# Batch 1's local attention by key sets of one alignment, with exponentials as the stationary operand

## The chip, the cores and the metric

The kernel runs on one core of a Trainium2 chip. The metric is the device time of one execution in microseconds (us), lower is better. The engines of a core are TensorE (PE, matrix products, with its weight loads counted apart as PEld), VectorE (DVE), ScalarE (ACT), GpSimd (POOL) and SyncE (SP). Each works through a queue of its own; POOL, SP and ACT also issue transfers (DMAs).

## What is computed

Eight batches of eight heads, 512 local and 32 global tokens a head, head size 64. Global queries attend to all 544 keys; a local query attends to the 32 global keys and to the local keys at most 32 positions away. The result, laid out as 4352 rows of 512, goes through a two-layer network with a quick GELU.

```python
k_all = concat([k_g, k_l]); v_all = concat([v_g, v_l])
out_g = softmax(q_g @ k_all.T / 8) @ v_all
s_ll = where(|i - j| <= 32, q_l @ k_l.T / 8, -1e9)
out_l = softmax(concat([q_l @ k_g.T / 8, s_ll])) @ v_all
x = concat([out_g, out_l]).transpose(0, 2, 1, 3).reshape(4352, 512)
h = x @ w_in                      # 512 -> 2048
out = (h * sigmoid(1.702 * h)) @ w_out
```

## The kernel before

**Units.** A "quad" is four heads of one batch (u = 0 or 1), one in each 32-partition row group of PE; a batch has two, `a` and `c`. The code runs in `tc.manual_schedule()` (line 54): every engine issues its instructions in the order in which the program text writes them. PSUM is two pools: `psS`, two tiles of two banks each (`spair`, line 288, always the same two), and `psP`, four single banks under one tag (line 61, `pbank`), which hold "hp" (first layer), "op" (second layer), "ov" (values) and others in turn; a bank is handed on when the last reader of its tile is done.

**Two ways of attention.** Batches 0 and 1 use `Quad` (line 294). Keys are in four windows of 128 (`WIN`, line 192), and the queries' columns are interleaved. `Tk` and `Tq` turn keys and queries on DVE, `ext` copies the global queries in, `S` forms scores (two rounds, 16 products each), `gg` and `K` the products with global keys, `X` and `XK` take exponentials on ACT, `M` multiplies by a mask on DVE, `ekUs` and `U` form three units of 512 columns (the row sums and two halves of the values) with values or ones as stationary operand, `Gm` the global queries' output, `R` and `XL` turn the sums and divide. Batches 2 to 7 use `Wide` (line 537). Here the values are the moving operand and the exponentials the stationary one. Keys are in sets that start at any multiple of 32, so `spread` (ACT, line 547) puts the turned keys into groups of 96 with 32 columns left free for the global keys, which `ext` (DVE, line 561) fills by transposes together with the global queries. `turn_v` (line 99) makes two shifted copies of the values by DMAs on SP, one for each other alignment. `S` takes 56 products a round, `UG` (line 597) 22 products a head into three "ov" banks, `RXG` (line 616) divides on DVE and turns the result into `xL` and `xG`.

**Order of the work.** Batch 0's attention and first layer come first (to 32.5 us). Then batch 0's second layer, 16 steps of four products (`osteps`, line 800; (t, f) is token tile t, quarter f of the 2048), is written out by hand with batch 1's attention between the steps (lines 804 to 851). Then batch 1's first layer (lines 856 to 878): 16 chunks of four 512-column products, each followed by a tanh on ACT (line 652) and a multiply on DVE (line 653); into it go the turning of batch 2's `a` quad, `turn_v(2)` and `a.S(0)`, `a.X(0)`. From then on `phase_o(i)` (line 880, the second layer of batch i with the next batch's attention) and `phase_h(i)` (line 940, a first layer) alternate. In `phase_o(1)` the `c` quad of batch 2 is turned too.

**Loads.** POOL issues them, mostly at the start in `load_rest` (line 258): batch 0's values, `w_in`, `w_out` in groups of four chunks, batch 1's queries and keys, part of batch 2's. After batch 0 come `load_v(2)`, the wide masks (`mask_rest`, `mask_blocks`, POOL) and `load(3)`. Batch 1's mask, `near_mask`, is made by four ACT copies in batch 0's first layer (`make_near`, line 209).

Of the kernel before, what the change touches and what calls it, by code (L numbers as in the profile page):

```python
# [20 lines left out]
def kernel(  # L21
# [67 lines left out]
    def load_v(b):  # L89
        vt = v_rows(b)  # L90
        if b < 4:
            nc.gpsimd.memset(vt[:, :, :, D:], 1.0)
# [4 lines left out]
        nc.gpsimd.dma_start(out=vt[0:32, 5, :, :D], in_=vs[480:512])  # L97

# [11 lines left out]
    rvg = consts.tile([128, 4, D + 2], BF16)  # L110


    rvt = consts.tile([128, 4, D + 2], BF16)
# [5 lines left out]
    def load_g(lo, hi, names="kqv"):  # L119
        for name, dst, src in (("k", rkg, kgf), ("q", rqg, qgf)):  # L120
            if name in names:
                nc.gpsimd.dma_start(out=dst[:, lo:hi, :], in_=src[:, lo:hi, :])
        if "v" in names:
            load_turned(nc.gpsimd, rvg[:, lo:hi, :D], vgf[:, lo:hi, :])
# [36 lines left out]
    for i in range(2):  # L161
        vtiles.append(consts.tile([128, 8 * 6 * (D + 2)], BF16, name="v%d" % i))
        nc.gpsimd.memset(v_view(i, 4)[:, :, :, :, D:], 1.0)
# [22 lines left out]
    for i in range(4):  # L186
        qt = consts.tile([128, 24, 32], F32, name="q%d" % i)
        nc.vector.memset(qt[:, 0:4, :], 0.0)
        nc.vector.memset(qt[:, 20:24, :], 0.0)
# [3 lines left out]
    near_mask = consts.tile([128, 2, LW], BF16)  # L193
# [15 lines left out]
    def make_near(c):  # L209
        nr = WIN[c][1]  # L210
        at = (0, 160, 0, 192)[c]
        nc.scalar.activation(near_mask[:, c // 2, at : at + 16 * nr].rearrange("p (t r) -> p t r", t=16),
                             near(bandt, c), AF.Copy)

# [5 lines left out]
    def mask_put(g, first, last, by, late):  # L220
# [22 lines left out]
    qgT = consts.tile([128, 4, 40], F32)  # L243
    nc.vector.memset(qgT[:, :, 32:], 0.0)
    kgT = consts.tile([128, 4, 32], F32)
# [12 lines left out]
    def load_rest():  # L258
# [13 lines left out]
        load(1, (1,))  # L272
        load(2, kq=False)
        nc.gpsimd.dma_start(out=loaded[2][1][:, 0], in_=qf[2][:, 0])
        load_g(4, 8, "k")
        load_v2(1)
        load_g(4, 8, "q")
        nc.gpsimd.dma_start(out=loaded[2][0], in_=kf[2])
        nc.gpsimd.dma_start(out=loaded[2][1][:, 1], in_=qf[2][:, 1])
# [14 lines left out]
    class Quad:  # L294
        def __init__(self, Q):
# [5 lines left out]
            self.v = v_view(self.b, 4 if self.b < 2 else 5)[:, self.u]  # L301
            if self.b < 2:
# [43 lines left out]
        def S(self, rnd, split=False, added=False, part=None):  # L346
# [19 lines left out]
            if not part:  # L366
                self.E[rnd] = att.tile([128, 4, RW + 32], BF16, name="e%d" % rnd)
# [29 lines left out]
        def M(self, rnd):  # L397
            at = 36 if rnd else 40
            e = self.E[rnd][:, :, at : at + LW]
            nc.vector.tensor_mul(e, e, near_mask[:, rnd : rnd + 1, :].to_broadcast([128, 4, LW]))  # L400

# [25 lines left out]
        def XK(self, two=True):  # L427
            self.ek = att.tile([128, Sl], BF16, name="ek")
            nc.scalar.activation(self.ek, self.kb, AF.Exp, scale=scale)
            self.ek2 = None  # L430
            if two:
                self.ek2 = att.tile([128, Sl], BF16, name="ek2")
                load_turned(nc.sync, self.ek2, self.ek)

        def ekU(self, unit, warm=0, ov=None):
# [4 lines left out]
            for j in range(4):  # L440
                two = unit == 1 and self.ek2 is not None
                r = 32 * ((j + 1 + two) % 4)
                p = slice(r, r + 32)
                lv = (ones32[p] if unit == 0 else
                      (rvt if two else rvg)[p, self.Q, :D].rearrange("p (w h) -> p w h", h=2)[:, :, unit - 1])
                nc.tensor.matmul(ov[32 * j : 32 * j + 32, :], lhsT=lv, rhs=(self.ek2 if two else self.ek)[p],
                                 start=True, stop=False, skip_group_check=True)

        def ekUs(self, nxt=None, rnd=0, banks=(None, None, None)):
# [5 lines left out]
            if self.ek2 is not None:  # L455
                self.ekU(1, ov=banks[1])
            if nxt:
                nxt.K(1)
            if self.ek2 is None:
                self.ekU(1, ov=banks[1])  # L460
# [76 lines left out]
    class Wide(Quad):  # L537
# [30 lines left out]
        def S(self, rnd):  # L568
# [14 lines left out]
            self.E[rnd] = att.tile([128, 4, LW], BF16, name="e%d" % rnd)  # L583
# [13 lines left out]
        def UG(self):  # L597
            self.ov = []
            for lo, hi in self.BANKS:
                ov = pbank("ov")  # L600
                self.ov.append(ov)
                work = []
# [208 lines left out]
    a.S(0)  # L811
    a.gg()
    a.K()
    a.X(0)
    a.XK()
    a.M(0)
    a.eg()
# [177 lines left out]
```

## Time and profile before

| | us |
|---|---|
| three runs | 297.93, 302.67, 298.87 |
| their median | 298.87 |
| the profiled execution | 297.81 |
| its span, first to last instruction | 295.9 |
| batch 0's second layer with batch 1's attention | 32.45 to 53.64 |
| batch 1's first layer | 53.64 to 69.00 |
| phase_o(1) | 69.00 to 89.89 |
| phase_o(2), for comparison | 103.71 to 122.17 |

The profiled execution is 1.9 us longer than its span, and 1.06 us below the median of the runs. In the lines of a profile, L670 is line 670 of the kernel; "op<-w_out_sb,gT" is output from inputs by the program's names. "x12" counts instructions. In the page's groups the first time is the sum, the second the mean of one in ns, and behind the second bar stands the idle time ahead of them and what ended it. The chain of work that ended last has start, length and what ran, in order of time. The timeline has start, length, engine, line, operation, and in brackets idle time with its releaser.

### The profile page before, as it was taken

How to read it: one execution, taken by the hardware profiler on the slowest of the kernel's cores; microseconds unless marked ns; L12 is line 12 of the kernel's file. 1: busy time of each engine (PE TensorE's matmuls, PEld its weight loads, DVE VectorE, ACT ScalarE, POOL GpSimd, SP SyncE). 2: the span in 40 equal slices, each digit the busy share in tenths (PEclk: the TensorE clock that was granted, in tenths of full speed). 3: DMA queues.
4: the chain of work that ended last, by engine and by line, in shares of the span. 5: the costliest groups of instructions: out<-in, count | busy, mean ns of one | idle time of the engine just before them, and what ended most of it. 6: DMA issues, size and time to landing. Idle time of an engine off the chain costs nothing.

```text
span 295.9 us, 9633 instructions
## 1 busy us (share of the span) xinstructions
PE 286.8 (97%) x4129; PEld 145.2 (49%) x4129; DVE 200.6 (68%) x409; ACT 161.5 (55%) x282; POOL 81.9 (28%) x143
## 2 busy tenths in 40 slices
PE   7899999999899999999999999999999999999995
PEld 6454445444444455444554445445544454455553
DVE  6578957987867776787768768777678644773220
ACT  4838475485536746575546734765556551663421
POOL 8742754781933500910063003600000000000000
PEclk9999999999999999999999999999999999999999
DMA  6999999979999992996289213950226012101123
GB/s 191 177 207 210 204 181 231 132 155 206 132 194 218 224 155 65 124 208 144 50 100 208 51 40 55 172 143 12 64 58 182 2 42 70 38 0 35 40 56 86
DMA packets 62874, 35.94 MB, mean 121 GB/s; under 512 B 49776, under 2 KB 51184, under 8 KB 62832
## 3 DMA queue, kind: packets, MB, share of 16 engines
q0 software_dynamic: 52752, 17.77, 53.9%
q1 hardware_dynamic: 9600, 16.91, 20.9%
q8 instruction: 32, 0.52, 0.7%
q10 hardware_dynamic: 480, 0.66, 0.7%
q14 instruction: 10, 0.08, 0.1%
HBM read 36.70 MB, written 8.91 MB: 154 GB/s over the span
## 4 chain that ended last, share of the span: by engine, by line
PE 89%; DVE 4%; DMA 2%; ACT 2%; issue 1%; SPq 0%; ACTq 0%; DVEq 0%
PE hp L645 38%; PE op L670 38%; PE s L578 4%; PE ov L611 3%; DMA g32k<-in_k_g_dram 2%; PE s L645 1%; PE s L360 1%; DVE xL L505 1%; PE ov L472 1%; PE op L682 1%; ACT e L393 1%; DVE rs L500 0%; DVE gT L653 0%; DVE e L593 0%; DVE sT L496 0%
## 5 line engine op out<-in xcount | busy, mean ns | idle before, releaser
L670 PE MATMUL op<-w_out_sb,gT 128*128 128x512 bf16 x528 | 123.7, 380 | 0.0
L653 DVE SCALAR_TENSOR_TENSOR gT<-th,hp 128x512 bf16<-128x512 f32 (+1 forms) x140 | 90.5, 655 | 35.1 <-ACT th L652 34.0
L645 PE MATMUL hp<-xL,w_in_sb 128*128 128x512 bf16 x496 | 109.0, 379 | 0.3 <-DVE xL L505 0.2
L652 ACT ACTIVATE th<-hp 128x512 f32<-128x512 f32 (+1 forms) x140 | 79.1, 572 | 42.8 <-PE hp L645 42.1
L645 PEld LDWEIGHTS <-w_in_sb 128*128 128x128 bf16 x576 | 56.2, 98 | 64.8 <-issue 1.1
L670 PEld LDWEIGHTS <-gT 128*128 128x128 bf16 x528 | 48.4, 98 | 52.2 <-issue 0.9
L587 ACT ACTIVATE e<-s 128x704 bf16<-128x704 f32 x48 | 33.7, 754 | 23.9 <-PE s L578 23.9
L95 POOL DMA_DIRECT2D v<-in_v_l_dram x30 | 23.6, 786 | 83.8 <-PE ov L611 69.9
L684 ACT ACTIVATE ob<-op 128x512 f32<-128x512 f32 (+2 forms) x35 | 20.5, 585 | 45.6 <-PE op L670 39.2
L593 DVE TENSOR_TENSOR e<-e,mask 128x1024 bf16<-128x1024 bf16 (+1 forms) x24 | 17.4, 725 | 24.3 <-ACT e L587 24.3
L625 DVE TENSOR_TENSOR xn<-ov,rc 128x384 bf16<-128x384 f32 (+1 forms) x36 | 19.5, 542 | 1.3
L96 POOL DMA_DIRECT2D v<-in_v_g_dram x30 | 17.7, 591 | 6.0 <-DMA rk<-in_k_l_dram 4.9
L578 PEld LDWEIGHTS <-kT 32*128 32x128 bf16 x1344 | 12.4, 92 | 10.9 <-issue 10.1
L578 PE MATMUL s<-q,kT 32*128 32x32 bf16 (+2 forms) x1344 | 15.4, 184 | 0.6 <-issue 0.6
L393 ACT ACTIVATE e<-s 128x856 bf16<-128x856 f32 x14 | 11.7, 882 | 6.0 <-PE s L360 6.0
L624 DVE RECIPROCAL rc<-ov 128x6 f32<-128x6 f32 (+1 forms) x36 | 6.5, 181 | 10.0 <-PE ov L611 10.0
L611 PEld LDWEIGHTS <-e 128*32 128x32 bf16 (+1 forms) x1056 | 10.0, 94 | 6.6 <-issue 2.5
L557 DVE STREAM_TRANSPOSE q<-rq 128x512 f32<-128x512 f32 x12 | 12.5, 1038 | 0.0
L544 DVE STREAM_TRANSPOSE kl<-rk 128x512 f32<-128x512 f32 x12 | 12.4, 1036 | 0.0
L611 PE MATMUL ov<-vt,e 128*32 128x66 bf16 x528 | 10.5, 195 | 1.4 <-DVE e L593 1.4
L611 PE MATMUL ov<-v,e 128*32 128x66 bf16 (+1 forms) x528 | 11.0, 197 | 0.0
L645 PE MATMUL hp<-xG,w_in_sb 128*128 128x256 bf16 x64 | 9.6, 273 | 0.0
(108 smaller groups left out, 176.0 us busy)
## 6 DMA issues: line engine op xcount, KB each, us to landing
out_dram<-ob SPq DMA_DIRECT2D x132, 64.0 KB, 2.5
vt<-v SPq DMA_DIRECT2D x12, 264.0 KB, 7.5
rk<-in_k_l_dram POOLq DMA_DIRECT2D x6, 512.0 KB, 12.2
vt<-v SPq DMA_DIRECT2D x6, 495.0 KB, 5.7
v<-in_v_l_dram POOLq DMA_DIRECT2D x30, 96.0 KB, 4.6
rq<-in_q_l_dram POOLq DMA_DIRECT2D x5, 512.0 KB, 10.8
w_out_sb<-in_moe_w_out_dram POOLq DMA_DIRECT2D x4, 512.0 KB, 10.6
rq<-in_q_l_dram POOLq DMA_DIRECT2D x5, 256.0 KB, 8.8
```

What stands on the lines that cost most here:

```text
L95: nc.gpsimd.dma_start(out=vt[0:96, c, :, :D], in_=vs[96 * c : 96 * c + 96])
L96: nc.gpsimd.dma_start(out=vt[96:128, c, :, :D], in_=vg)
L578: nc.tensor.matmul(bank(self.ps, j)[:, 0:LW].rearrange("p (t q) -> p t q", q=32)[:, os], lhsT=self.k[p, k0 : k0 + 128, e], rhs=self.q[p, t ...
L587: nc.scalar.activation(self.E[rnd][:, 2 * i : 2 * i + 2, :], self.ps[i][:, :, :LW], AF.Exp, scale=scale)
L593: nc.vector.tensor_mul(e, e, m.to_broadcast([128, 4, n]))
L611: nc.tensor.matmul(ov[32 * j : 32 * j + 32, 66 * to : 66 * to + 66], lhsT=self.E[rnd][0:n, j, 32 * o : 32 * o + 32], rhs=self.vs[rho][0:n, ...
L625: nc.vector.tensor_mul(xn[:, lo // 2 : hi // 2].rearrange("p a h w b -> p a b h w"), o3[:, 0:n, 0:D].rearrange("p (a b) (w h) -> p a b h w ...
L645: nc.tensor.matmul(hp[:, : width(i)], lhsT=w_in_c[:, fc // 8, kc, fc % 8 // 2, :, fc % 2], rhs=(xL[i] if i < B else xG)[:, kc, :], start=( ...
L652: nc.scalar.activation(th[:, :n], hp[:, :n], AF.Tanh, scale=0.851)
L653: nc.vector.scalar_tensor_tensor(gTs[i][:, fc, :n], in0=th[:, :n], scalar=1.0, in1=hp[:, :n], op0=ALU.add, op1=ALU.mult)
L670: nc.tensor.matmul(op, lhsT=gTs[i][:, fc, tci * 128 : tci * 128 + 128], rhs=w_out_sb[:, fc, :], start=(first and fc == 4 * f4), stop=(fc = ...
L684: nc.scalar.activation(ob[:, lo:hi], op[:, lo:hi], AF.Copy, scale=0.5)
```

## The change

Batch 1 gets a class `Near`, derived from `Wide`. All its key sets have the one alignment (starts at multiples of 128 in the spread keys), so that it needs no shifted copies of the values. At the seams between sets a query block takes two products instead of one: 32 products a head instead of 22 in `UG`. `S` has 32 and 48 products a round, with 512 columns of scores; `XM` takes the exponential of half a round (1024 elements) on ACT and multiplies it by the mask on DVE. `near_mask` has a new layout and is made on POOL by `mask_near`, in the middle of the loads. Batch 1's values are loaded by `load_v(1)`, and the order of the loads behind `load_g(2, 4)` is new. The order of `osteps` and attention is rewritten. All exponentials lie in one buffer `ebuf`. `a.UG()` takes three banks of `psP`, `c.UG(spair())` three of `psS`. Batch 1's first layer begins with four banks instead of two. Batch 2's turning moves: `a.Tq` from batch 1's attention into that first layer, `turn_v(2)` from chunk 8 to 4, and in `phase_o(1)` `c.spread` behind `a.X(1)`, `c.Tq` behind `a.M(1)`, and `a2.Tk`, `a2.spread` behind `a.RXG`. The diff, cut to what matters:

```diff
     def load_v(b):
         vt = v_rows(b)
+        if b == 1:
+            nc.gpsimd.memset(vt[:, 5], 0.0)
...
+        if b == 1:
+            nc.gpsimd.dma_start(out=vt[96:128, 5, :, :D], in_=vs[480:512])
...
+    ebuf = consts.tile([128, 8192], BF16)
...
+    def mask_near():
+        def zero(lo, hi, first, last, by):
+            nc.gpsimd.memset(near_mask[lo:hi, first:last:by], 0.0)
+
+        nc.gpsimd.memset(near_mask, 1.0)
+        zero(0, 96, 4, 24, 5)
+        zero(0, 96, 24, 27, 1)
+        for g, first, late in ((1, 0, True), (0, 1, False), (2, 1, True), (1, 2, False), (2, 3, False), (0, 4, True)):
+            mask_put(g, first, 24, 5, late, near_mask)
+        zero(64, 96, 0, 24, 5)
+        zero(0, 32, 2, 24, 5)
+        zero(0, 64, 3, 24, 5)
+        mask_put(3, 24, 25, 1, True, near_mask)
...
             if g4 == 0:
                 load(1, (0,))
                 load_g(2, 4)
-        load(1, (1,))
-        load(2, kq=False)
-        nc.gpsimd.dma_start(out=loaded[2][1][:, 0], in_=qf[2][:, 0])
-        load_g(4, 8, "k")
-        load_v2(1)
-        load_g(4, 8, "q")
-        nc.gpsimd.dma_start(out=loaded[2][0], in_=kf[2])
-        nc.gpsimd.dma_start(out=loaded[2][1][:, 1], in_=qf[2][:, 1])
+                mask_near()
+                load(1, (1,))
+        load_v(1)
+        load_g(4, 8)
+        load(2)
...
+    NEAR = (
+        ((0, 0, 5, 0), (128, 3, 5, 5), (128, 17, 1, 15), (256, 6, 5, 10)),
+        ((384, 9, 5, 0), (384, 17, 1, 14), (512, 12, 5, 5), (512, 17, 1, 15), (256, 17, 1, 13), (544, 15, 3, 10)),
+    )
+
+    class Near(Wide):
+        def S(self, rnd):
+            self.ps = spair()
+            for k0, lo, n, o in NEAR[rnd]:
+                for e in range(2):
+                    for j in range(4):
+                        p = slice(32 * j, 32 * j + 32)
+                        nc.tensor.matmul(
+                            bank(self.ps, j)[:, 32 * o : 32 * o + 32 * n],
+                            lhsT=self.k[p, k0 : k0 + 128, e], rhs=self.q[p, lo : lo + n, :, e],
+                            start=(e == 0), stop=(e == 1), skip_group_check=True,
+                        )
...
+        def XM(self, rnd):
+            lo, n, at = ((1, 14, 0), (0, 13, 14))[rnd]
+            m = near_mask[:, at : at + n].rearrange("p (a t) q -> p a (t q)", a=1)
+            for i in range(2):
+                e = self.E[rnd][:, 2 * i : 2 * i + 2]
+                nc.scalar.activation(e, self.ps[i], AF.Exp, scale=scale)
+                e = e[:, :, 32 * lo : 32 * lo + 32 * n]
+                nc.vector.tensor_mul(e, e, m.to_broadcast([128, 2, 32 * n]))
+
+        def parts(self, t):
+            if t == 16:
+                return [(0, 0, 0, 0, 128), (0, 15, 0, 1, 96), (1, 13, 0, 2, 96), (1, 14, 0, 3, 96),
+                        (1, 15, 0, 4, 96), (1, 12, 0, 5, 128)]
+            work = []
+            for m in range(5):
+                d = t - 3 * m
+                if -1 <= d <= 3:
+                    o = (d + 1 if m == 0 else 5 * m + d + 1 if m < 3 else 16 + 5 * (m - 3) + d + 1)
+                    work.append((o // 16, o % 16, 0, m, 128 if 0 <= d < 3 or t == 15 else 96))
+            if t >= 14:
+                work.append((1, t - 4, 0, 5, 128))
+            return work
...
-        if fc in (5, 6, 8, 9):
-            make_near((5, 6, 8, 9).index(fc))
...
-    nq = {1: (Quad(2), Quad(3)), 2: (Wide(4), Wide(5))}
+    nq = {1: (Near(2), Near(3)), 2: (Wide(4), Wide(5))}
     a, c = nq[1]
-    a.T()
-    transpose_g(2, 4)
+    a.Tk()
+    a.spread()
+    a.Tq()
     a.ext()
-    osteps(0, (0, 1), (0, 0), (1, 1), (1, 0), (2, 1))
+    osteps(0, (0, 1), (0, 0), (1, 1))
     a.S(0)
...
+    a.XM(0)
+    c.Tk()
+    osteps(0, (1, 0), (2, 1), (2, 0))
+    a.S(1)
+    c.spread()
+    a.XM(1)
+    c.Tq()
     c.ext()
...
+    osteps(0, (3, 1), (3, 0), (0, 2))
     c.S(0)
...
+    c.XM(0)
+    osteps(0, (0, 3), (1, 2), (1, 3))
     c.S(1)
...
+    c.XM(1)
+    osteps(0, (2, 2))
+    a.UG()
+    a.RXG()
+    osteps(0, (2, 3), (3, 2))
+    c.UG(spair())
+    c.RXG()
+    osteps(0, (3, 3))
...
-    hps = [pbank("hp") for _ in range(2)]
-    for fc, kcs in ((0, (0, 1)), (1, (0, 1)), (0, (2, 3)), (1, (2, 3))):
-        h_mm(1, fc, hps[fc], kcs)
+    hps = [pbank("hp") for _ in range(4)]
+    for kcs in ((0, 1), (2, 3)):
+        for fc in range(4):
+            h_mm(1, fc, hps[fc], kcs)
     for fc in range(FC):
...
         if fc == 2:
             a.Tk()
+        if fc == 4:
+            a.spread()
+            turn_v(2)
         if fc == 5:
-            a.spread()
+            a.Tq()
...
         if i == 1:
-            c.T()
-            c.spread()
+            c.Tk()
         a.S(1)
         a.X(1)
+        if i == 1:
+            c.spread()
         a.M(1)
         if i == 1:
+            c.Tq()
             c.ext()
-        if n < B:
+        elif n < B:
             a2.Tk()
         o(0)
         a.UG()
-        if n < B:
+        if i > 1 and n < B:
             a2.spread()
         a.RXG()
+        if i == 1:
+            a2.Tk()
+            a2.spread()
         o(1, 0, 1)
         c.S(0)
         c.X(0)
```

## The prediction

> **What bounds the kernel now.** I read the engine table first, then the chain of work that ended last, then the timeline of the stretch that the change rewrites (30 to 90 us).
>
> ```profile
> PE 286.8 (97%) x4129; PEld 145.2 (49%) x4129; DVE 200.6 (68%) x409; ACT 161.5 (55%) x282; POOL 81.9 (28%) x143
> PEclk9999999999999999999999999999999999999999
> L593 DVE TENSOR_TENSOR e<-e,mask 128x1024 bf16<-128x1024 bf16 (+1 forms) x24 | 17.4, 725 | 24.3 <-ACT e L587 24.3
> ```
>
> PE is the bound, at full granted clock. A change gains where it takes work from PE, and loses where PE comes to a product before its operands. The chain, from the end of batch 0's first layer:
>
> ```profile
> 32.61 4.32 PE op L670 x20
> 36.93 0.60 PE s L360 x16
> 37.53 0.15 PE s L379 x8
> 37.68 0.46 PE kb L379 x7
> 38.14 2.70 PE op L670 x12
> 40.83 0.60 PE s L360 x16
> 41.44 1.83 PE op L670 x8
> 43.27 0.60 PE s L360 x16
> ...
> 83.95 0.87 PE ov L611 x81
> ```
>
> Batch 1's attention is cut into batch 0's second layer ("op"). Its short products take 36.93 to 38.14, two times 0.60, 45.70 to 48.06 and 49.89 to 51.90: 6.8 us. A run of 12 op products takes 2.70 us, of 8 1.83, of 4 about 0.95.
>
> ```profile
> 34.54 1.03 DVE L317 STREAM_TRANSPOSE kT<-rk 128x512 f32<-128x512 f32 x1
> 36.27 0.49 DVE L331 COPY q<-qgT 128x40 f32<-128x40 f32 x4
> 36.86 0.67 PE L360 MATMUL s<-q,kT 32*128 32x200 bf16 x16
> 72.02 0.60 ACT L551 ACTIVATE kT<-kl 128x480 f32<-128x480 f32 x1 [2.31 <-DVE kl L544]
> 72.65 1.38 ACT L587 ACTIVATE e<-s 128x704 bf16<-128x704 f32 x2
> 74.95 0.24 PE L611 MATMUL ov<-vt,e 128*32 128x66 bf16 x8 [1.40 <-DVE e L593]
> ```
>
> The reader sees two things. The first scores of batch 1 start at 36.86, right behind DVE's turning (34.54 to 36.76): 20 op products fill PE until then. And at 72 ScalarE's spread waits 2.31 us for DVE while ready scores queue behind it; PE pays 1.5 us (73.5 to 74.95). Each engine keeps its written order.
>
> **PE's work.** Scores: Near has 512 columns a round, times two for the halves of the contraction, 32 and 48 products. The old round (856 columns, 16 products) took 0.60, the wide one (704 columns, 56 products) 0.57. By columns alone that gives 0.63, by products (0.57/56 x 80) 0.82; I take 0.70, as the columns are the nearer measure. Values: 22 products per head now take 0.87 (L611, 88 records); 32 take 32/22 x 0.87 = 1.27 or, with the 0.26 that is not streaming kept fixed, 1.14; I take 1.2. Batch 1 then costs 4 x 0.70 + 2 x 1.2 = 5.2 against 6.8: **-1.6** (-1.0 to -2.0).
>
> **Three new waits of PE in batch 1.** I walk the queues in written order, with rows for the durations.
>
> First, a.S(0). DVE is free at 34.5 as before (its gT operations end 34.6; they follow PE's 32.6, not the four near-mask copies that leave ScalarE at 24.5 to 28.5). Tk to Tq start is 0.90 (70.94 to 71.84), Tq to the end of ext 1.30 (80.11 to 81.41); the spread (0.6 and 0.2) lies beside Tq. Scores can start at 36.8, as before. But only 12 op products stand ahead now: PE is free at 35.1 and waits **1.7**.
>
> Second, c.S(0). a.S(0) to 37.5, 12 op to 40.2, a.S(1) to 40.9, 12 op to 43.6: PE is there. Operands: exponentials of 1024 elements from 37.6, each some 0.95 to 1.0 (L393 takes 0.88 for 856), end 39.5; multiply 0.6, to 40.2; c.Tk behind it to 41.1; c.spread to 41.8, and only then a.XM(1)'s exponentials, to 43.7, though their scores were there at 41.0; multiply to 44.35; c.Tq and ext behind it, 1.30, to 45.6. PE waits **2.0**.
>
> Third, a.UG's third bank. The pool has four PSUM banks; op tiles 2 and 3 are still open there, so the third "ov" can only take the bank of the first, once DVE has done its reciprocal and multiply (0.2 + 0.6). c.S(0) 45.6 to 46.3, 12 op to 49.0, c.S(1) to 49.7, 4 op to 50.7, two banks of values to 51.4. ScalarE evicts op tile 1 (49.1 to 49.7), then c.XM(1) to 51.75; DVE multiplies to 52.35, then turns to the first bank: free at 53.15. PE waits **1.75**; that DVE operation is also what c.RXG and h(1) queue behind.
>
> Then: third bank to 53.65, 8 op to 55.5, c.UG to 56.7 (other pool, no wait), 4 op to 57.6. c.RXG (2.83 from first reciprocal to xL, 76.06 to 78.89) starts when c's first bank is there, 55.9, and ends 58.7. PE has 8 products on u = 0 to 59.3, so the old wait there (53.64 to 55.22 for 4 to 5 products, 0.7 lost) is covered: **-0.7**. Layer one is 64 x 0.216 = 13.8 and a.S(0) 0.57; all four banks are taken at its start and DVE has 0.65 per chunk plus 2.5 for Tk, Tq and ext, so PE waits about 0.5. It ends at 57.6 + 13.8 + 0.6 + 0.5 = 72.5; before, at 69.0: **+3.5**, the sum of the terms above plus 0.1 for one more switch and rounding.
>
> **Batch 2's turning (phase_o(1)).** It takes 20.9 (69.00 to 89.89); the same phase of the next batch 18.5 (103.71 to 122.17). a.X(1) no longer queues behind the spread: M(1) ends 3.7 after the start, and values come at 4.1, so the 1.5 goes. Late next: a2.Tk now stands behind c.Tq, ext and a.RXG on DVE (ext ends 4.9, RXG lasts 2.95, Tk ends 8.75), and a2.spread stands on ScalarE ahead of c.X(0). Those exponentials run 9.4 to 10.8 instead of 8.1 to 9.5; c.S(1) needs their PSUM and PE is there at 9.2. It waits **1.6**. So 18.5 + 1.6 = 20.1, **-0.8** of which 0.65 is one idle in PE at 86.8 put down to issue, which may come back: 0 to -0.8.
>
> **Loads and small edits.** POOL's mask_near is 13 short operations, some 4 us (memset 128x576 0.60, tensor_scalar 32x224 0.37, copies 0.23 each). It falls at 20.6 to 24.7, where POOL now waits 1.85 and 1.80 for transfers to land before it may issue more; eight are under way then (four of 512 KB, two of 256 and two small ones), so the queues don't run dry. Behind it: k, q of u = 1 (needed at 40, land near 35), w_out groups 2 and 3 (land 2.5 later than 35.3 and 37.9; needed at 43 and 46). load_v(1) is 12 issues for 4 and two memsets; paced by landings as now, the last is issued near 43 and lands near 47, for 50.7. Batch 2's k, q land near 55, needed at 62; its values are issued some 4 us later than now and turn_v(2), moved up on SP, waits for them, with cover to 76. SP sheds four turned copies; nothing queues behind turn_v until the next outputs. All nothing; if cover fails, it is the late-values rival. Dropped memsets, copies and the output's other row order: nothing, beside PE.
>
> **Sum.** +3.5 - 0.8 = +2.7 on the profiled 297.81 (span 295.9, 1.9 around it): 300.5. The median of the three runs is 1.06 above that execution, which would give 301.6. I say **301.0**.
>
> **Rivals.** *The turning comes in time* (faster). If Tk, spread, Tq, ext end before PE asks, at a.S(0) and c.S(0), 1.7 + 2.0 go: 301.0 - 3.7 = 297.3. For it: ScalarE loses 2.07 us of near-mask copies ahead of the last tanh. Against: that tanh waits for PE (0.2 to 0.3 each), not ScalarE. It decides once the two waits add to under 1.0.
>
> *Values late*: batch 1's last loads take the 10.6 that the slowest such load took (42.75), landing 53.5 instead of 47; the third bank then waits further and c.UG after it: about +1.5, 302.5. Against: the rows from 50 on land in 3.6 to 5.6.
>
> *The work doesn't shrink* (the change doesn't do what it says): per product, not per column, 5.8 against 6.8, and 0.65 of issue wait for 320 more PE instructions: 302.3. For it: 56 products of few columns cost almost what 16 long ones did.
>
> *A wait slows the clock*: if the wait at c.S(0) is long enough that PE's granted clock falls to half behind it, the 12 op products there take 5.4 instead of 2.7: +2.7, 303.7. Against: no slice of before shows less than full clock, but its longest wait in this stretch is 1.5. [...]
>
> **Numbers.** The forecast 0.60 (its own range 299.5 to 302.5), turning in time 0.15, values late 0.10, work not less 0.10, slower clock 0.05. From 297.0 to 303.5 all but the last and the tails of the others lie inside. About 2% is what a measurement can tell from no change (292.9 to 304.8): none of the cases lies below, the clock case with late values lies above: faster 0.02, same 0.93, slower 0.05.
>
> **What would show it.** Right: PE idle ahead of a.S(0), c.S(0) and inside a.UG, released by ext, ext, and the multiply on the first bank; a.S(1) of batch 2 near 72.5; c.X(0) of batch 2 behind a spread. Wrong: a.S(0) before 36, c.S(0) right behind 12 op products, the three banks in one run, or score rounds over 0.8. The forecast fails most easily if DVE and ScalarE don't keep the written order.

## The result

The change makes the kernel slower: 308.5 us median (307.67 to 311.21, four runs) against 298.56 (297.93 to 302.67, four runs), a ratio of 1.0356 [1.027, 1.0441]. The forecast was 301.0, with 303.5 as the upper end of the range: wrong by 7.5 us. The profiled execution of the changed kernel took 309.15, its span 307.4.

The page of the changed kernel, with the lines that answer to those of before, and the queue that carries instructions (packets, MB, share of the DMA engines' time):

```profile
PE 288.7 (94%) x4289; PEld 145.4 (47%) x4289; DVE 200.1 (65%) x403; ACT 161.2 (52%) x278; POOL 89.5 (29%) x162
PEclk9999997899999999999999999999999999999999
q8 instruction: 33, 0.54, 0.8%
L588 DVE TENSOR_TENSOR ebuf<-ebuf,mask 128x1024 bf16<-128x1024 bf16 (+1 forms) x24 | 17.4, 724 | 24.3 <-ACT ebuf L582 24.3
```

PE is busy for 1.9 us longer although it has less to compute, and two slices (46 to 61 us) show 7 and 8 tenths of its clock, where the kernel before has only nines. Where the time lies, by stages of the two profiled executions (from the first second-layer product of batch 0 to the first first-layer product of batch 1; from there to the first second-layer product of batch 1; from there to the first first-layer product of batch 2):

| us | before | after | difference | forecast |
|---|---|---|---|---|
| up to batch 0's second layer | 32.45 | 33.92 | +1.5 | 0 |
| batch 0's second layer with batch 1's attention | 21.19 | 30.64 | +9.4 | +4.0 |
| batch 1's first layer | 15.93 | 16.14 | +0.2 | -0.5 |
| batch 1's second layer, phase_o(1) | 20.17 | 20.66 | +0.5 | -0.8 |
| the rest of the span | 206.15 | 206.09 | -0.1 | 0 |

The stage that the change rewrites carries it. Its chain in the changed kernel (start, length, what ran):

```profile
47.13 0.66 PE s L644 x27
47.80 4.38 PE op L710 x12
52.18 0.70 PE s L644 x46
...
56.21 0.53 PE ov L606 x42
56.73 2.18 issue
58.91 0.30 PE ov L606 x8
59.21 3.36 PE op L710 x8
62.57 1.18 PE s L606 x127
```

Before, 12 op products took 2.70 and 8 took 1.83. Here they take 4.38 and 3.36, and in the middle of a.UG PE stands for 2.18 us with nothing to wait for in the records ("issue"). The timeline of PE and DVE in that stage shows the three forecast waits, each behind the DVE operation named:

```profile
37.88 0.30 DVE L560 STREAM_TRANSPOSE kT<-rkg 128x160 f32<-128x160 f32 x1
38.32 0.67 PE L644 MATMUL s<-q,kT 32*128 32x160 bf16 x32 [1.65 <-DVE kT L560]
41.61 0.70 PE L644 MATMUL s<-q,kT 32*128 32x160 bf16 x48
46.69 0.30 DVE L560 STREAM_TRANSPOSE kT<-rkg 128x160 f32<-128x160 f32 x1
47.13 0.66 PE L644 MATMUL s<-q,kT 32*128 32x160 bf16 x32 [2.12 <-DVE kT L560]
55.57 0.58 DVE L620 TENSOR_TENSOR xn<-ov,rc 128x384 bf16<-128x384 f32 x1
56.21 0.53 PE L606 MATMUL ov<-v,ebuf 96*32 96x66 bf16 x44 [1.67 <-DVE xn L620]
58.91 0.30 PE L606 MATMUL ov<-v,ebuf 96*32 96x66 bf16 x8 [2.18 <-issue]
```

The same stretch by windows (busy time of PE, PEld, DVE, ACT, POOL with instructions in brackets, then the granted clock, DMA share and GB/s):

```profile
47.10:50.00 2.90, 2.87 (x40) 1.47 (x41) 0.83 (x2) 2.17 (x3) 2.90 (x6) 0.76 1.15 102
50.00:51.50 1.50, 1.50 (x5) 0.46 (x4) 0.42 (x1) 0.26 (x1) 1.50 (x4) 0.50 1.14 187
58.90:62.30 3.40, 3.39 (x16) 1.18 (x16) 1.56 (x5) 0.60 (x1) 2.65 (x8) 0.50 1.39 107
```

PE is busy, but at half its clock: in the trace from 48.62 and from 58.86, for 3.41 us each. So three waits of 1.65, 2.12 and 1.67, two half-rate windows that cost 1.68 and 1.53, and 2.18 without instructions; less the shorter PE work.

### The profile page after: what moved, and what is told of

Its sections match the earlier page's. It is cut to its first block, busy times and chain, and to the rows that moved or that the text cites. A ratio compares the mean times of both kernels' runs of the same rounds, so it can differ in the third digit from the quotient of the medians.

```text
span 307.4 us, 9954 instructions
## 1 busy us (share of the span) xinstructions
PE 288.7 (94%) x4289; PEld 145.4 (47%) x4289; DVE 200.1 (65%) x403; ACT 161.2 (52%) x278; POOL 89.5 (29%) x162
## 4 chain that ended last, share of the span: by engine, by line
PE 79%; DVE 7%; DMA 5%; ACT 5%; issue 2%; POOL 1%; ACTq 0%; POOLq 0%
PE op L710 34%; PE hp L685 34%; PE s L572 4%; PE ov L606 3%; DMA w_in_sb<-in_moe_w_in_dram 3%; DMA rk<-in_k_l_dram 2%; DVE gT L693 2%; ACT ebuf L658 2%; DVE kl L538 1%; DVE q L551 1%; PE s L685 1%; ACT th L692 1%; DVE xn L620 1%; PE op L722 1%; PE s L644 1%
## 5 line engine op out<-in xcount | busy, mean ns | idle before, releaser
L710 PE MATMUL op<-w_out_sb,gT 128*128 128x512 bf16 x528 | 127.1, 387 | 0.0
L693 DVE SCALAR_TENSOR_TENSOR gT<-th,hp 128x512 bf16<-128x512 f32 (+1 forms) x140 | 90.6, 656 | 35.5 <-ACT th L692 34.7
L692 ACT ACTIVATE th<-hp 128x512 f32<-128x512 f32 (+1 forms) x140 | 78.8, 572 | 43.7 <-PE hp L685 43.3
L97 POOL DMA_DIRECT2D v<-in_v_l_dram x35 | 27.6, 787 | 90.1 <-PE ov L606 82.4
L582 ACT ACTIVATE ebuf<-s 128x704 bf16<-128x704 f32 x48 | 33.7, 754 | 23.5 <-PE s L572 21.3
L588 DVE TENSOR_TENSOR ebuf<-ebuf,mask 128x1024 bf16<-128x1024 bf16 (+1 forms) x24 | 17.4, 724 | 24.3 <-ACT ebuf L582 24.3
L98 POOL DMA_DIRECT2D v<-in_v_g_dram x35 | 20.7, 591 | 9.2 <-DMA rk<-in_k_l_dram 7.2
L606 PEld LDWEIGHTS <-ebuf 128*32 128x32 bf16 (+1 forms) x1312 | 12.4, 94 | 11.6 <-issue 7.3
L606 PE MATMUL ov<-v,ebuf 128*32 128x66 bf16 (+1 forms) x656 | 12.8, 197 | 5.1 <-issue 3.5
L545 ACT ACTIVATE kT<-kl 128x480 f32<-128x480 f32 x14 | 8.4, 598 | 9.4 <-DVE kl L538 9.4
L660 DVE TENSOR_TENSOR ebuf<-ebuf,near_mask 128x896 bf16<-128x896 bf16 (+1 forms) x8 | 4.9, 609 | 10.2 <-ACT ebuf L658 10.2
L606 PE MATMUL ov<-vt,ebuf 128*32 128x66 bf16 x528 | 10.4, 195 | 0.0
```

What stands on the lines that cost most here:

```text
L97: nc.gpsimd.dma_start(out=vt[0:96, c, :, :D], in_=vs[96 * c : 96 * c + 96])
L98: nc.gpsimd.dma_start(out=vt[96:128, c, :, :D], in_=vg)
L582: nc.scalar.activation(self.E[rnd][:, 2 * i : 2 * i + 2, :], self.ps[i][:, :, :LW], AF.Exp, scale=scale)
L606: nc.tensor.matmul(ov[32 * j : 32 * j + 32, 66 * to : 66 * to + 66], lhsT=self.E[rnd][0:n, j, 32 * o : 32 * o + 32], rhs=self.vs[rho][0:n, ...
L692: nc.scalar.activation(th[:, :n], hp[:, :n], AF.Tanh, scale=0.851)
L693: nc.vector.scalar_tensor_tensor(gTs[i][:, fc, :n], in0=th[:, :n], scalar=1.0, in1=hp[:, :n], op0=ALU.add, op1=ALU.mult)
```

## The experiments

The theory after the result: the waits are as forecast; a wait, or a stretch without instructions, can be followed by half the clock (it was behind the second wait, 2.12 us, and behind the third with the idle on issue, 1.67 and 2.18, and not behind the first, 1.65); and PE ran out of instructions, because its short products pass faster than the queue of instructions is refilled beside the loads. The rivals: the waits alone move (no second cause), or instructions cost only their own time. Fifteen kernels; each ratio is to the kernel before, run beside it on the same chip.

**Work in the second wait.** Nine products of zeros, 512 columns each, into the bank that c.S(0) then starts anew:

```diff
-    c.S(0)
+    c.S(0, 9)          # nine zero products ahead of the scores
```

> The changed kernel with nine 512-column products on zeros put ahead of c.S(0), in the PSUM that c.S(0) is about to write: they take up PE's second new wait (2.1 us) and move nothing else. Theory (the waits of PE lower its clock): the granted clock stays at 1.00 behind c.S(0), the 12 op products there take 2.7 us instead of 4.4, and the time falls by 1.7 us, or by up to 3.4 if the second half-rate stretch goes too. Rival (Near's many short products lower the clock themselves): two half-rate stretches as before, no change in time. Rival (the loss is the loads and the start): no change.

Measured 306.53 (305.52 to 307.84), ratio 1.0299 [1.0241, 1.0356]. The 12 op products behind c.S(0) ran at full clock (2.76; one record is missing), and the window near 50 us was gone (granted clock 1.00 from 47.1 to 51.0); the one near 58 stayed (0.994 in the mean of the profile), with 2.40 us on issue:

```profile
46.74 2.76 PE L711 MATMUL op<-w_out_sb,gT 128*128 128x512 bf16 x11
56.39 0.43 PE L606 MATMUL ov<-v,ebuf 96*32 96x66 bf16 x17 [2.40 <-issue]
```

c.S(0) came as late behind the start of the stage as in the changed kernel (13.1 and 13.2 us), and the stage took 29.08 instead of 30.64. So some 1.6 us of the loss in this stage came from the clock alone.

**Short fillers in the first two waits.** 26 products of 128 columns ahead of a.S(0), 26 of 160 ahead of c.S(0):

> The changed kernel with 26 products of 128 columns ahead of a.S(0) and 26 of 160 columns ahead of c.S(0), on zeros, into PSUM that is about to be written. They take up the first and second wait and put 104 more instructions into PE's stream ahead of c.S(1), so that the place at which a.UG stands still for 2.2 us with nothing to wait for in the profile (8 products before its end) falls elsewhere. Theory (PE's instructions come in blocks of 256, fetched by a transfer that a full DMA queue delays): the 2.2 us idle leaves its place in a.UG and mostly hides behind the third wait; with the clock whole behind c.S(0) the time falls by some 4 us against the changed kernel, 2 more than with the fill of the second wait alone. Rival (the idle comes from the values' loads or another operand): it stays 8 products before the end of a.UG, and the time is that of the fill of the second wait alone.

Measured 307.1 (304.85 to 308.13), ratio 1.0293 [1.0233, 1.0353]. With 52 more products the idle on issue moved: 0.55 us in a.UG, 2.26 in c.UG, and 1.39 and 0.59 in phase_o(1). It follows the count of instructions, not the piece of work, as the theory has it. The time did not: of the 4 us forecast, 1.4 came, since the idle went to c.UG and phase_o(1) and kept a half-rate window behind it (the profile's mean granted clock is 0.994).

The position can be counted. Over all records of PE from the first (products, weight loads and a few others, 14 in the changed kernel), the idle on issue stands behind record 1473 and 2753 in the changed kernel, behind 2497 in the kernel before (its 0.65 at 87.46), and behind 1473, 1729 and 2753 in all_waits_out_spread_back (below). These are whole multiples of 256 apart, in three kernels with different work at these places.

**The second wait removed.** c's keys and queries turned ahead of the output steps:

```diff
     a.ext()
+    c.Tk()
+    c.Tq()
     osteps(0, (0, 1), (0, 0), (1, 1))
     a.S(0)
     a.XM(0)
-    c.Tk()
+    c.spread()
+    c.ext()
...
-    c.spread()
     a.XM(1)
-    c.Tq()
-    c.ext()
```

> The changed kernel with c.Tk and c.Tq ahead of a.XM(0) on VectorE, and c.spread and c.ext behind a.XM(0), so ahead of a.S(1). Theory (the second wait is the written order of VectorE and ScalarE): no wait ahead of c.S(0), clock at 1.00 behind it, a.XM(1) 2 us earlier; the time falls by 2.1 + 1.7 = 3.8 us, up to 6 if the second half-rate stretch goes too. Rival (keys and queries of the second quad land too late for any order): c.Tk waits for its load and the time falls by less than 1 us.

Measured 308.1 (307.23 to 308.91), ratio 1.0336 [1.0293, 1.0379]. The wait of 2.12 is gone, and the time is not (3.8 less was forecast, 0.4 came):

```profile
43.89 0.66 PE L644 MATMUL s<-q,kT 32*128 32x160 bf16 x32
51.27 0.52 PE L606 MATMUL ov<-v,ebuf 96*32 96x66 bf16 x44 [1.67 <-DVE xn L620]
55.03 0.30 PE L606 MATMUL ov<-v,ebuf 96*32 96x66 bf16 x8 [3.24 <-issue]
```

c.S(0) starts at 43.89 without a wait, and a.UG then has 3.24 us on issue, with two half-rate windows from 53.01 on. A gain of 2 turned into another stall. In the trace, the packets of the instruction queue explain the idle: a fetch of 16 KB ended at 53.66, and PE went on at 55.03. (The changed kernel has 33 such fetches for 8578 products and weight loads of PE, some 260 instructions each.)

**The same with the loads later.** Eighteen clears of a scratch tile keep POOL busy between V(1)'s issues and the next batch's loads:

```diff
         load_v(1)
+        for _ in range(18):
+            nc.gpsimd.memset(scratch, 0.0)
         load_g(4, 8)
         load(2)
```

> The order of turn_c_early, with 18 clears of a small scratch tile on POOL between the issues of V(1) and those of the next batch's gathered rows, q and k, so that those loads and V(2)'s behind them begin some 10 us later; nothing else differs. In turn_c_early a.UG idled 3.24 + 0.33 us on issue at 51.8, and the block of 256 PE instructions it waited for was fetched at 52.64 to 53.66, 4.3 us after the border before it; two windows of half clock (6.83 us) began at 53.01. Theory (the block's fetch queues behind the loads' transfers): the fetch follows its border by some 1 to 2 us, a.UG idles under 0.8 us on issue, at most one window of half clock is left, and the time falls by 3 to 5 us against turn_c_early, to 303 to 305. Rival (the fetch comes when it comes, whatever the loads do): idle and time as in turn_c_early, 307 to 309. Later loads that come too late for h(1) or phase_o(1) would show as waits for V(2)'s or batch 2's turned rows between 64 and 85 us.

Measured 307.16 (306.31 to 309.55), ratio 1.0325 [1.0258, 1.0391]: the time is the rival's, the trace the theory's.

```profile
44.53 10.43 POOL L287 MEMSET scratch<- 128x512 bf16 x18
51.64 0.59 PE L609 MATMUL ov<-v,ebuf 96*32 96x66 bf16 x52 [1.67 <-DVE xn L623]
55.48 0.31 PE L609 MATMUL s<-v,ebuf 96*32 96x66 bf16 x16 [0.37 <-issue]
66.08 1.03 DVE L541 STREAM_TRANSPOSE kl<-rk 128x512 f32<-128x512 f32 x1 [4.42 <-DMA rk<-in_k_l_dram]
67.69 2.82 PE L688 MATMUL hp<-xL,w_in_sb 128*128 128x512 bf16 x8 [4.56 <-DVE gT L696]
```

The idle on issue fell from 3.24 in a.UG and 0.92 in c.UG to 0.37 in c.UG, the half-rate windows before 60 us are gone (11 records of op products in 2.76 us from 44.85, 16 of h(1) in 3.62 from 56.60), and h(1) started at 56.60 instead of 62.34: 5.7 us won. All of it went in h(1), where DVE waited 4.42 us for batch 2's keys, which the clears had put off, and PE 4.56 behind it.

In five kernels, from the trace: when PE passed the border between two blocks that lies 256 records ahead of the stall, when the next block was fetched, and when PE went on.

| | border before | fetch | PE goes on | idle on issue |
|---|---|---|---|---|
| after | 52.6 | 56.68 to 57.62 | 58.91 | 2.18 |
| turn_c_early_loads_later | 52.0 | 52.84 to 53.98 | 55.48 | 0.37 |
| before_320_more_products (below) | 47.5 | 51.63 to 52.59 | 54.02 | 2.23 |
| all_waits_out_spread_back (below) | 48.6 | 52.84 to 53.71 | 55.08 | 2.50 |
| change_fewer_products (below) | 49.7 | 53.62 to 54.57 | 56.08 | 0.17 |

PE goes on 1.3 to 1.5 us after its block has landed. With the loads moved away the fetch began 0.9 us after the border; beside them, 4.0 to 4.2. So PE could go on 3.5 us behind the border without the loads and 6.3 to 6.5 beside them, and the idle is what PE did not need of that time for its own work and its other waits.

The loads can hold the fetch up and need not: in the first 105 us of six profiles (both kernels, all_waits_out_spread_back, before_new_phase_o1_spread_later and the two of all waits out with later loads) the fetch began at most 1.35 us behind its border at the 7 borders behind which the queue of the loads moved nothing for 1 us, and up to 5.0 us behind it at the 62 others.

**More instructions in the kernel before.** 80 small products of zeros behind `ekU(2)` in each of batch 1's quads:

```diff
+            if self.Q in (2, 3):
+                for n in range(80):
+                    j = n % 4
+                    nc.tensor.matmul(self.st[0][32 * j : 32 * j + 32, 0:66], lhsT=warm[:, 0:32], rhs=warm[:, 0:66],
+                                     start=False, stop=False, skip_group_check=True)
```

> The kernel before with 160 small products of zeros (32 x 128 by 128 x 66, four groups of columns, 80 for each of batch 1's quads, added into a bank that is being summed, so that no value changes): 320 more PE instructions in batch 1, as many as the change has there, and no other wait. Theory (blocks of 256 instructions pass faster than they are fetched beside the loads): the work itself, 160 by some 10 ns in chains of four, 1.6 us or less, plus 1 to 3 us of issue idle behind a border near the products: 1.5 to 4.5 us slower, 299.4 to 302.4. Rival (instructions cost only their own time): 0.5 to 1.6 us slower.

Measured 305.59 (304.98 to 307.06), ratio 1.0264 [1.0225, 1.0304]: 7.2 us more, above both forecasts, at full clock all through the profiled execution (mean granted clock 1.000).

```profile
54.02 0.75 PE L465 MATMUL s<-warm 128*32 128x66 bf16 x71 [2.23 <-issue]
57.85 0.25 PE L495 MATMUL og<-v,e 128*32 128x66 bf16 x8 [2.10 <-issue]
```

Two idles of 2.23 and 2.10 appear in a kernel that had none there; the products themselves take about 0.65 a quad. The stage grew by 5.9 (27.12 against 21.19), phase_o(1) by 2.3 (22.47 against 20.17). So 320 short instructions alone, without any of the change's waits, cost 5.9 us in the stage in which the change lost 9.4.

**Fewer instructions in the changed kernel.** The order stays; of 32 value products a head 12 are left out (the second ones at the seams and four for the global queries), 96 products in all. Those parts of the weighted sums are missing.

```diff
             if t == 16:
-                return [(0, 0, 0, 0, 128), (0, 15, 0, 1, 96), (1, 13, 0, 2, 96), (1, 14, 0, 3, 96),
-                        (1, 15, 0, 4, 96), (1, 12, 0, 5, 128)]
+                return [(0, 0, 0, 0, 128), (1, 12, 0, 5, 128)]
...
-            return work
+            return [x for x in work if x[4] == 128]
```

> The changed kernel (308.5) with the same 96 products left out, and its order as it is. Its three waits stay. Theory: a.UG's idle on issue (2.18 us) goes or shrinks to under 0.7, and the half-rate window behind it (1.55 us) may go with it, as the third bank's wait of 1.7 us alone leaves PE idle for about half of a window; with 0.9 us of work: 303.5 to 306. Rival (instructions cost only their work): 307.4 to 308.

Measured 303.39 (301.88 to 304.03), ratio 1.0163 [1.0113, 1.0214]: 5.1 below the change, for 0.9 of work.

```profile
45.91 0.67 PE L644 MATMUL s<-q,kT 32*128 32x160 bf16 x32 [2.12 <-DVE kT L560]
46.51 2.76 PE L709 MATMUL op<-w_out_sb,gT 128*128 128x512 bf16 x11
53.30 0.43 PE L606 MATMUL ov<-v,ebuf 128*32 128x66 bf16 x32 [1.93 <-DVE xn L620]
56.08 0.58 PE L606 MATMUL s<-v,ebuf 128*32 128x66 bf16 x49 [0.17 <-issue]
```

The three waits are all there (1.65, 2.12, 1.93). The idle on issue is 0.17, both half-rate windows are gone (the profile's granted clock is 1.0), and the stage takes 24.79; the forecast had 25.0 for it, 24.1 without the 0.9 of work left out. In this stage it is nearly the kernel that the prediction described. The whole is not: the profiled execution, 301.88, is 2.3 above the 299.6 that the forecast gives for it (300.5 less 0.9), with 0.5 of that in this stage, 0.9 in h(1) and 1.0 behind phase_o(1).

**All waits out.** c turned early, five steps ahead of a.S(0), three between the later pieces, c.S(0) right before a.UG (output tiles 0 and 1 are done by then, so its three banks are free), and in phase_o(1) a2.spread behind c.X(0):

```diff
-    osteps(0, (0, 1), (0, 0), (1, 1))
+    c.Tk()
+    c.Tq()
+    osteps(0, (0, 1), (0, 0), (1, 1), (1, 0), (2, 1))
...
     c.S(0)
+    a.UG()
+    a.RXG()
     c.XM(0)
-    osteps(0, (0, 3), (1, 2), (1, 3))
+    osteps(0, (2, 3))
     c.S(1)
     c.XM(1)
-    osteps(0, (2, 2))
-    a.UG()
-    a.RXG()
-    osteps(0, (2, 3), (3, 2))
+    osteps(0, (3, 1), (3, 0), (3, 2))
     c.UG(spair())
```

> The changed kernel in another order: c's turning (Tk, Tq) ahead of the output products, five output steps ahead of a.S(0), c's spread and extension right behind a's first exponentials, three steps behind them, a.S(1) three steps before a.UG, c.S(0) just before a.UG, and in phase_o(1) a2's spread behind c's first exponentials. The waits of 1.65, 2.12 and 1.67 us, and the 0.73 + 0.46 us at c.S(1), should go, and with them the two half-rate windows (1.7 + 1.55 us): 9.3 us in all, 299 against the 308.5 of the changed kernel. If the block fetches then stop a.UG and c.UG as they did in turn_c_early (3 to 4 us), 302 to 304. Rival (the waits only move, since VectorE's work sets the end): 306 to 309.

Measured 300.68 (299.46 to 309.35, six runs), ratio 1.0084 [1.0046, 1.0122]. The profiled execution was the 309.35, 8.7 above the median, so its lines are not used. The gain of 7.8 is near the forecast; but a kernel with all three waits gone, and by the forecast 1.6 us less work for PE, is still not faster than before.

**The same, a2's spread where the change has it.**

> The order of all_waits_out with a2's spread of phase_o(1) back where the change has it; the rest as there. Theory: the wait of some 1.2 us at c.S(1) comes back, partly paid for by less idle on issue in c.UG behind it (1.97 us in the profile of all_waits_out): 0.3 to 1.2 us above all_waits_out, 301 to 302. Rival (instruction fetch sets the pace of phase_o(1), the wait is free): the same time, 300.3 to 301.

Measured 302.93 (301.01 to 303.64), ratio 1.0157 [1.0126, 1.0188]: 2.2 more, above the 0.3 to 1.2 forecast.

```profile
48.61 0.22 PE L644 MATMUL s<-q,kT 32*128 32x96 bf16 x4 [1.04 <-issue]
55.08 0.31 PE L606 MATMUL s<-v,ebuf 96*32 96x66 bf16 x16 [2.50 <-issue]
83.48 0.19 PE L572 MATMUL s<-q,kT 32*128 32x32 bf16 x2 [0.72 <-ACT ebuf L582]
```

This profile shows what is left in batch 1: no wait for an engine, 3.54 us on issue and a half-rate window behind the second (mean granted clock 0.994). The stage takes 23.52 against 21.19 before.

**All waits out, fewer products.** The same 96 products left out of all_waits_out:

> all_waits_out without the second products at the seams and four of the six for the global queries: 20 value products a head instead of 32, 96 products (192 PE instructions) fewer in batch 1. It leaves out those parts of the weighted sums. Theory: the work itself is some 0.9 us (two quads of 12/32 x 1.2), and the idle on issue in batch 1 falls by another 1.5 to 3 us: 297 to 298.5. Rival (the instructions cost only their work): 299.5 to 300.

Measured 297.93 (295.61 to 304.0, ten runs), ratio 0.9982 [0.9948, 1.0015]: 2.75 below all_waits_out, as the theory had it. The stage takes 19.07, with no idle on issue in it. The number of instructions, then, and not the order, is what all_waits_out had left in this stage.

**All waits out, loads 5.6 us later, and 7.8 us later** (ten clears; fourteen, with batch 2's turning two rounds later in h(1)):

> The order of all_waits_out (300.68 against 298.36 before) with ten clears of a scratch tile on POOL between V(1)'s issues and those of the next batch's gathered rows, q and k: those loads and V(2)'s begin some 5.6 us later. The profile of all_waits_out had issue idles of 4.01 us at 50.8, 0.88 at 60.9, 0.85 at 88.0 and 1.97 at 93.6, and two half-rate windows at 52.5. Theory (the fetch of the next PE instructions queues behind the loads): the first idle falls to under 1.5 us and its half-rate windows go, with perhaps 1 us of wait for batch 2's k in h(1): 296 to 299. Rival (the idle moves to the next border, as in the earlier runs): 299 to 302.

> As the run before, with 14 clears (7.8 us), and batch 2's first turning in h(1) two rounds later (k at chunk 4, spread and values at 6, q at 7, extension at 8, scores at 11), so that VectorE does not stand before k's landing. Theory: issue idle in a.UG and c.UG of batch 1 under 1 us together, no half-rate window before 80 us: 295 to 298. Rival: the scores at chunk 11 come too late for phase_o(1), whose a.UG then waits 1 to 2 us, or V(2) lands late: 298 to 301.

Measured 302.9 (301.08 to 306.55), ratio 1.0151 [1.01, 1.0202], and 303.77 (301.5 to 308.01), ratio 1.0159 [1.0117, 1.0201]. Both missed. In batch 1 they did what they were for: 0.83 and 0.32 us on issue instead of 3.54, the stage 21.08 and 20.39. But h(1) took 19.24 and 20.07, where all_waits_out_spread_back has 17.41 and the changed kernel 16.14, behind batch 2's late keys (DVE waited 3.03 and 3.12 for them, PE 3.17 and 2.74 behind it):

```profile
48.98 0.22 PE L647 MATMUL s<-q,kT 32*128 32x96 bf16 x4 [0.83 <-issue]
63.59 2.75 PE L688 MATMUL hp<-xL,w_in_sb 128*128 128x512 bf16 x12 [3.17 <-DVE gT L696]
```

At none of the three delays tried did the later loads cost nothing.

**Values bank by bank.** all_waits_out with an output step between a.UG's three banks, the same products in all:

```diff
     c.S(0)
-    a.UG()
-    a.RXG()
     c.XM(0)
+    a.UG(ks=(0,))
+    osteps(0, (2, 2))
+    a.UG(ks=(1,))
     osteps(0, (2, 3))
+    a.UG(ks=(2,))
+    a.RXG()
```

> The order of all_waits_out (300.68; its later run with a2's spread put back showed the same stretch undisturbed), but a.UG's three banks apart, an output step of four long products between them, c.S(1) one step behind the third bank, three steps, then c.UG. No product more or less. Theory (blocks of 256 PE instructions pass faster than the fetch): spread out, the blocks pass in 4 to 6 us instead of 2.3 to 3.8, and the idles on issue in batch 1, 1.04 and 2.50 us in the last profile, fall to under 1.2 us together: 1.5 to 3 us less than all_waits_out, 297.5 to 299. Rival (the idle comes with the short products wherever they stand): 300 to 302.

Measured 302.54 (300.16 to 306.66), ratio 1.0139 [1.0079, 1.0199]: above even the rival's 302. a.UG ran without idle, and c.UG had 2.19 us on issue at 53.2, its block fetched at 53.06, 3.8 us after the border before. Spread out in one place, the products met the stall at the next dense one.

**phase_o(1) alone, in the kernel before.**

> The kernel before with the change's order in phase_o(1) alone: c's k turned ahead of a.S(1), c's spread behind a.X(1), c's q and extension behind a.M(1), a2's k and spread behind a.RXG. My forecast for this part was 0.8 us less, with 0 to 0.8 as the spread: the wait of 1.5 us at a.M(1) goes, a new one of some 1.2 to 1.6 us comes at c.S(1). Measured inside the changed kernel phase_o(1) took 0.5 us more than before. So against the kernel before: 297.0 to 297.9 by the forecast; by the changed kernel's profile 298.4, if the issue idle in c.UG comes with it.

Measured 297.57 (296.79 to 298.86, ten runs), ratio 0.9972 [0.9946, 0.9999]: 0.8 less by the medians, the forecast. In the profile the stage took 19.80 against 20.17, so 0.4 less, with the new wait at c.S(1) (0.72 + 0.45 behind a2's spread) in it.

**And with a2's spread behind c's exponentials.**

```diff
         if i == 1:
             a2.Tk()
-            a2.spread()
         o(1, 0, 1)
         c.S(0)
         c.X(0)
+        if i == 1:
+            a2.spread()
```

> The kernel before with the change's order in phase_o(1), and there a2's spread and extension of keys behind c's first exponentials instead of ahead of them. In the changed kernel c.S(1) waited 0.73 + 0.46 us for those exponentials behind a2's spread on ScalarE. Theory: that wait goes, so some 0.5 to 1.2 us less than before_with_new_phase_o1 (297.57): 296.4 to 297.1. Rival: the products wait for instructions there instead (idle on issue in c.UG grows), and the time stays at 297.3 to 297.8.

Measured 296.52 (295.78 to 304.53, twelve runs), ratio 0.9959 [0.9933, 0.9985]: the fastest version here, 0.4% ahead of the kernel before.

```profile
77.54 1.41 ACT L587 ACTIVATE e<-s 128x704 bf16<-128x704 f32 x2 [2.84 <-PE s L578]
78.83 0.61 ACT L551 ACTIVATE kT<-kl 128x480 f32<-128x480 f32 x1
79.25 0.63 PE L578 MATMUL s<-q,kT 32*128 32x32 bf16 x56
```

The exponentials now start as soon as the scores are there, the spread follows, and c.S(1) runs in one piece. The stage takes 17.94.

**The ones of V(1) set again** (a small clear that the change had dropped):

> The changed kernel with the one memset given back that it dropped on GpSimd ahead of the first loads (the ones beside the second values buffer, 0.12 us), so that the loads of batch 0's second quad are issued 0.08 us later, as before the change. Theory (the 1.5 us by which batch 0's first layer starts later come from these loads going ahead of the second half of batch 0's early queries): the first layer's last products start at 22.1 instead of 23.6, the time falls by 1.4 us. Rival (the start varies from run to run): no change in time.

Measured 308.22 (307.24 to 308.69), ratio 1.0336 [1.0294, 1.0378]: no difference from the change. Batch 0's second layer began at 32.58 here and between 32.50 and 33.23 in the profiles of the other experiments, with or without the clear (that of all_waits_out again apart); the 33.92 of the changed kernel's profile is taken as a property of that execution.

## Why the prediction was wrong

**The three waits: right.** Forecast 1.7, 2.0 and 1.75, released by ext, ext and the multiply on the first bank; measured 1.65, 2.12 and 1.67, so released. Walking the queues in written order held to 0.1 us, and the stage, freed of the rest, took 24.79 against 24.1.

**PE's work: right.** Score rounds 0.66 to 0.71 in the timeline against 0.70, value rounds 1.18 for c.UG against 1.2. (The price by products, "0.57/56 x 80", took the 80 products of both rounds for one; it went only into a rival, which it made too dear.)

**The clock: the first failed step.** The rival *a wait slows the clock* had 0.05, and the sum had nothing for it: that gaps of 1.7 to 2.0 us leave the clock whole was not shown by any row of before, whose longest wait from 30 to 90 us is 1.40. The runs show what counts instead. Half clock comes in whole stretches of 3.41 us that lie on one grid through the execution (in the profile of the change they start at 48.62, at 58.86 and, behind the last instruction, at 308.03: 3 and 73 lengths apart). In 16 profiles (all but that of all_waits_out), taking as idle the share of such a stretch in which no matmul record runs (from 5 us on, without the output's tail behind 285 us): all 11 stretches with 0.63 or more idle were followed by half clock; of the three from 0.57 to 0.61, one was; below that none that ran at full clock. (In the profile of all_waits_out one stretch with 0.55 idle was, so the limit is not sharp.) The wait of 2.12 fell into one stretch (from 45.20) with 1.93 of it, 0.57 idle: half clock. The same wait in change_fewer_products was cut in two by the grid: none (granted clock 1.0). So the length of a gap alone does not decide it: one gap of 2.12 us was enough, and so were two in one stretch, parts of the 1.67 and the 2.18 (2.88 us idle together in that from 55.44, 0.85 of it), while the wait of 1.65 had no half clock behind it (0.48 of its stretch, from 34.96, idle). The rival's price was too high (2.7; measured 1.68, about half of 3.41), and it struck twice.

**Instructions: the second failed step.** The prediction put "0.65 of issue wait for 320 more PE instructions" into the rival *the work doesn't shrink*, chance 0.10. Measured: 2.18 in a.UG and 1.28 in phase_o(1), and 4.33 for 320 instructions in the kernel before. The 0.65 on issue in the profile of before was the same stall at a small size (a block fetched at 85.11 to 86.07, PE on at 87.46, behind record 2497), and was not recognised:

```profile
87.46 0.60 PE L578 MATMUL s<-q,kT 32*128 32x96 bf16 x53 [0.65 <-issue]
```

The changed kernel's 33 packets of instructions for 0.54 MB are 16.4 KB each. At its stall in a.UG, PE passed the block ahead in 4.1 us, waits included (52.6 to 56.7), and the next one's fetch, beside the loads, began only 4.1 us behind the border (56.68). Twelve op products of 512 columns are 24 instructions in 2.7 us; a value round's are 256, 1.18 in c.UG.

These two explain the whole excess in the stage: 9.4 measured less 4.0 forecast is 5.4, and 2.18 + 1.68 + 1.53 is 5.4. change_fewer_products takes both away and stands at 303.39, its profiled execution at 301.88; what it has left over the forecast lies for the most part outside this stage, and no run here takes it apart.

**Loads: right and wrong.** "All nothing" held for every landing (no wait for a load is on the changed kernel's chain there). It left out that the same transfers hold up PE's instructions (fetches 4.0 to 4.2 us behind their border beside them, 0.9 with them moved away).

**h(1)** was forecast at -0.5 and came at +0.2: its 64 products of 0.216 and two score rounds of 0.57 make 15.0 of the 16.14, so PE lost some 1.2 us where 0.5 was forecast, with L692 and L693 (tanh and multiply) and batch 2's turning on the chain. **phase_o(1)**: the old wait went, the new one came at the place named, 0.73 + 0.46 instead of 1.6, and of the 0.65 on issue "which may come back", 1.28 did:

```profile
88.74 0.60 ACT L545 ACTIVATE kT<-kl 128x480 f32<-128x480 f32 x1 [3.79 <-DVE kl L538]
89.37 1.39 ACT L582 ACTIVATE ebuf<-s 128x704 bf16<-128x704 f32 x2
90.16 0.19 PE L572 MATMUL s<-q,kT 32*128 32x32 bf16 x2 [0.73 <-ACT ebuf L582]
90.80 0.61 PE L572 MATMUL s<-q,kT 32*128 32x32 bf16 x54 [0.46 <-ACT ebuf L582]
96.92 0.33 PE L606 MATMUL ov<-v,ebuf 128*32 128x66 bf16 x17 [1.28 <-issue]
```

Alone, in the kernel before, the part was worth the 0.8 forecast by the medians and 0.4 in the profiled stage.

**The sum.** Excess over the profile's 300.5: stage 5.4, h(1) 0.7, phase_o(1) 1.3, the start 1.5 (that execution's), -0.3 for the rest and around the span: 309.1; the profiled execution is 309.15.

What stays open: why the fetch starts as late as 4 us behind its border beside the loads. Moving the loads took the delay away, so they have a part in it; which of their packets stands in front, and why some fetches beside loads start at once, no run here shows.

## What to carry to other kernels

Price a wait of PE not only by its length: place it on the grid of 3.41 us, together with the other gaps near it, and add some 1.6 us (1.68 and 1.53 here) where about 0.6 of a window or more would be idle. Where long products are replaced by many short ones, count PE's instructions: here PE stood idle behind a block of 256 that it passed, waits included, in less than 6.3 to 6.5 us beside heavy loads (3.5 without them), and a wait removed ahead of it came back in part as a longer stall (2.18 to 3.24 in turn_c_early). A small "issue" idle in the profile, 0.65 here, is a warning of it.

## What the runs showed of the hardware

Half clock in whole windows of 3.41 us, after windows of which some 0.6 or more was idle (0.57 and 0.85 in the profile of the change, the first by the wait of 2.12 us alone). Instruction fetches of 16 KB per some 260 PE instructions (33 packets for 8578), which PE follows 1.3 to 1.5 us after they land, and which began at most 1.35 us behind the border with the queue of the loads empty and up to 5.0 us behind it beside them. Stalls at borders that lie whole multiples of 256 records apart (1473, 1729, 2497, 2753) in different kernels. Ten to eighteen clears of 128x512 on POOL, 0.58 us each (10.43 for 18), are a usable way to hold a queue of loads back in an experiment; what they hold back is then late elsewhere.
